# An attention and expert kernel: weighing of v by a list of pairs a slot, gates and expert choices at other places, six buffers of v

## The chip, the cores and the metric

The kernel runs on one core of one Trainium2 chip. Its time is the device time of one execution in microseconds (us); the time before is the median of three runs. One further execution was taken with the hardware profiler, and all durations below are from that one. Engines are named as the profile names them: PE is the matrix engine (PEld its weight loads), DVE the vector engine, ACT the scalar engine, POOL the GpSimd engine, SP the engine that issues most of the transfers. Each works through its own instructions in the order in which the program has them, and waits on semaphores for the others.

## The reference

Two blocks, the second fed by the first. Everything is float32.

```
scores = q @ k^T / sqrt(64)                      # (8 batches, 8 heads, 576, 576)
cum    = cumsum(max(s, 0))                       # (8, 8, 576)
scores = where(future, -1e9, scores + min(-(cum[i] - cum[j]), 0))
attn   = exp(scores - max);  attn /= sum(attn) + 1e-9
x      = heads of (attn @ v) side by side        # (8, 576, 512)

logits = x @ w_gate                              # 8 experts
local  = sigmoid(x @ w_local)
for b, s:  fresh = argmax(logits[b, s])
           e = fresh if s == 0 or local[b, s] < 0.5 else the e of the token before
           out[b, s] = softmax(logits[b, s])[e] * (relu(x[b, s] @ w1[e]) @ w2[e])
```

## The kernel before, in words

**Two stages.** The attention stage computes x and routes it: each token row of x is scattered to a table in device memory, ordered by expert. The expert stage takes units of up to 256 table rows that share an expert, multiplies them by that expert's w1 and w2, and scatters the results to the output.

**Attention by slots.** A *pair* n is two heads of one batch; there are 32, four a batch. The loop at L960 runs over 16 *slots* m of two pairs, 2m (even) and 2m + 1 (odd). In a slot PE first computes the scores of both pairs (`scores`, L854: tile `ps`, four parts a pair; ACT takes the exponential into `e`, POOL masks the diagonal blocks, L851), and then the values of both (`values`, L885). A pair's values come in two tiles, `po0` and `po6`, and each has one buffer. The sum over keys needs v weighed by the exponential of cum: `weigh(n)` (L837) writes it to one of four tiles `vg`, two DVE multiplications a pair (L845) and a small ACT copy (L842). v itself is loaded into `va`, of which there are four buffers (`p_v`, NV).

**Emptying and turning.** After each `po` tile DVE takes the reciprocal of the sums into `recs` (L902) and writes the scaled values to `xb` (L903). At a slot's end `turn` (L914) transposes both pairs into `xt` for the router, and then, before the change, `weigh` is called for the pairs 2m + 4 and 2m + 5.

**Places.** Other work is put into the slots by `plan(slot, place, f)`. Place 0 is after the even pair's scores, 1 after the odd pair's, 3 after the even pair's values, 4 after the odd pair's, 5 after turning and weighing. Since each engine keeps the program's order, the place decides what an instruction stands behind on its engine.

**The router.** Two batches form a group g, and there are four. With m = 4(g + 1), for the first three: `product` (PE, L213, at (m, 1)), `logits` (DVE, L222 to L231, at (m, 3)), `codes` and `turn1` (DVE, L238 to L267, at (m, 5)), `exps` (ACT, (m + 1, 1)), `turn2` (DVE, L274 to L289, (m + 1, 3)), `gates` (DVE, L321 to L332, (m + 1, 5)), `ranks` (PE, L297 and L298, (m + 2, 1)), `rows` (DVE, L306 to L313, (m + 2, 3)). Then the group's 18 scatters are laid out by the tuple STORES, whose entries are places, slot after slot from m + 2. A scatter is an indirect transfer that POOL issues (L345); at places 3, 4 and 5 a one-element copy of `recs` (L344) ahead of it makes POOL wait until DVE has got to that emptying. Scatters that STORES doesn't place go to the expert stage.

**Choosing units.** `assign_early(0)` and `assign_early(1)` (L407; `assign`, L376) choose the experts and rows of the first two and the next three units on DVE, from the counts so far: some 20 small instructions each. SP reads the result for the addresses of weights (`load`, L497) and rows (`fetch`, L517). The first stood at (10, 5), the second at (15, 0). The last group's first half has its product and logits at (14, 4). In the expert stage `run` (L613) has a list of its own: (u, c) is after the c-th column block of unit u's first layer.

**What holds buffers.** `xb` of batch 7 takes the buffer of batch 3, so its first emptying (pair 28, slot 14) waits for batch 3's scatters, the last of which is at (13, 5). The `kb` and `qb` of pairs 2m + 4 and 2m + 5 are requested inside slot m, behind a one-element DVE write (L762) that follows the emptying of the odd pair's `po0`.

Of the kernel before, what the change touches and what calls it, by code (L numbers as in the profile page):

```python
# [12 lines left out]
Alu = mybir.AluOpType  # L13
# [4 lines left out]
P = 128  # L18
B, H, S, DH = 8, 8, 576, 64
D = H * DH  # L20
E, F = 8, 1024
N = B * S
HP = H // 2
# [18 lines left out]
GB = 2  # L42
NG = B // GB
NC = GB * NJ
XW = 4 * 32 + 2
NV = 4
STORES = (((4, 5), (0, 1, 3, 4, 5), (0, 1, 3, 4, 5), (0, 1, 3, 4, 5), (0,)), ((4, 5, 5), (0, 1, 3, 4, 5), (0, 1, 3, 4, 5), (0, 1, 3, 4, 5)),
          ((4, 5), (0, 0, 1, 1, 3, 4, 5, 5)))
BX = 3
CAP = N + DH  # L50
ROWS = E * CAP + 2 * P
# [1 line left out]
DOUBLE, SINGLE, HALF, QUARTER = 2 * P, P, P // 2, P // 4  # L53
EARLY = (2, 3)
# [57 lines left out]
class Router:  # L112
# [294 lines left out]
    def assign_early(self, i):  # L407
        v = self.nc.vector
        self.counted()
        n = self.shifted("n0", 8)  # L410
        if i == 0:
            self.used, self.start, self.early = self.t("used", [P, E]), self.t("start", [P, E]), []
            v.memset(self.used, 0.0)
        v.tensor_tensor(n, n, self.used, op=Alu.subtract)
        v.tensor_scalar(self.start, self.used, float(DOUBLE), None, Alu.mult)
        of, used, _ = self.assign(f"a{i}", n, self.start, EARLY[i], DOUBLE)
        self.early.append(of)
        v.tensor_tensor(self.used, self.used, used, op=Alu.add)

    def assign_doubles(self):  # L420
        v = self.nc.vector
# [27 lines left out]
class Experts:  # L449
# [163 lines left out]
    def run(self, recs, wend, out_of):  # L613
        tc, ctx, nc, router = self.tc, self.ctx, self.nc, self.router
# [10 lines left out]
        last, first = NG - 1, sum(EARLY)  # L625
        self.banks = lambda name: self.ps_m.tile([P, 1, 512], F32, name=name, tag="m")

        def late_rows():
# [4 lines left out]
            self.puts += router.pads()  # L633

        todo = {
            (0, 2): [lambda: router.product(last, self.xts_of, self.banks, (1,)),
                     lambda: router.logits(last, (1,)), lambda: router.codes(last), lambda: router.exps(last),
                     lambda: router.turn1(last), lambda: router.turn2(last)],
# [17 lines left out]
            before[l] = two[i - 2] if i >= 2 else None  # L656
        self.load(1)
        self.turn_x(1)
        self.load(2)
        loaded, done, fetched, freed = [3, 3], (set(), set()), 2, False  # L660

        def ready(l, layer):
# [68 lines left out]
def attention(ctx, tc, q, k, v, s, wx, ident, recs, wend, router, experts):  # L731
# [4 lines left out]
    def pool(name, bufs, **kw):  # L736
        return ctx.enter_context(tc.tile_pool(name=name, bufs=bufs, **kw))

    once = pool("once", 1)
    p_in = pool("p_in", 4)  # L740
    p_v = pool("p_v", NV)
    p_e = pool("p_e", 2)
    p_x = experts.p_x
    p_x0 = pool("p_x0", 1)
# [21 lines left out]
    def load_v(n):  # L766
        if n >= NPAIR:
            return
        b, hp = divmod(n, HP)
        va = vs[n] = p_v.tile([P, NB, 2, DH], F32, name="va")  # L770
        nc.sync.dma_start(va.rearrange("p c h d -> p (c h d)"), v[b, hp].rearrange("p c h d -> p (c h d)"))
# [14 lines left out]
    load_qk(2)  # L786
    load_v(2)
    load_qk(3)
    load_v(3)
    router.projection(wx)  # L790
    wk = once.tile([P, NPAIR, G1 + NB, 2], F32, name="wk")
    nc.gpsimd.memset(wk[:TL, :, G1 + NF], 0.0)
# [44 lines left out]
    def weigh(n):  # L837

        if n >= NPAIR:
            return  # L840
        va, vg = vs.pop(n), vgs[n % NV]
        nc.scalar.copy(vg[:, :, :, VW - 2 : VW - 1].rearrange("p c h e -> p (c h) e"),  # L842
                       wk[:, n].rearrange("p c h -> p (c h)").unsqueeze(2))
        for to, c in ((slice(0, G1), G1), (slice(G1, G1 + NB), NB)):
            nc.vector.tensor_tensor(vg[:, to].rearrange("p c h e -> p (c h) e")[:, :, :DH],  # L845
                                    va[:, :c].rearrange("p c h e -> p (c h) e"),
                                    wk[:, n, to].rearrange("p c h -> p (c h)").unsqueeze(2).to_broadcast([P, c * 2, DH]),
                                    op=Alu.mult)
# [59 lines left out]
    def turn(n):  # L908

        b, hp = divmod(n, HP)  # L910
        bl = b % GB
        if hp == 0:
            xts[b] = (p_xt, experts.p_xt)[bl].tile([P, HP, 2, NJ, 32], F32, name=f"xt{bl}")
        nc.vector.transpose(xts[b][:, hp].rearrange("p d j t -> p j d t"), xs[b][:, :, :, 32 * hp : 32 * hp + 32])  # L914

    def of(g):
        return xts[g * GB], xts[g * GB + 1]

# [2 lines left out]
    def plan(slot, place, f):  # L921
        todo.setdefault((slot, place), []).append(f)

    for g in range(NG - 1):
        m = HP * GB // 2 * (g + 1)
        plan(m, 1, lambda g=g: router.product(g, of(g), banks))
        plan(m, 3, lambda g=g: router.logits(g))
        plan(m, 5, lambda g=g: (router.codes(g), router.turn1(g)))
        plan(m + 1, 1, lambda g=g: router.exps(g))
        plan(m + 1, 3, lambda g=g: router.turn2(g))  # L930
        plan(m + 1, 5, lambda g=g: router.gates(g, [xs[b] for b in range(g * GB, g * GB + GB)]))
        plan(m + 2, 1, lambda g=g: router.ranks(g, banks))
        plan(m + 2, 3, lambda g=g: router.rows(g))
        places = [(m + 2 + i, p) for i, ps in enumerate(STORES[g]) for p in ps]
        for c in range(NC):
            if c >= len(places):
                experts.puts.append(lambda after, g=g, c=c: router.scatter(g, c, after))
                continue
            i, p = places[c]
            after = {3: (2 * i, NJA), 4: (2 * i + 1, 0), 5: (2 * i + 1, NJA)}.get(p)  # L940
            after = after and recs[0:1, after[0], after[1], 0:1]
            plan(i, p, lambda g=g, c=c, after=after: router.scatter(g, c, after))
    m = NPAIR // 2
    plan(1, 5, router.constants)
    plan(2, 5, router.constants2)
    plan(2, 3, range_ends)
    plan(m - 6, 5, lambda: router.assign_early(0))
    for i in range(4):
        plan(m - 5 + i, 5, lambda i=i: experts.load(0, None, i))
    plan(m - 2, 0, lambda: (experts.fetch(0), experts.fetch(1)))  # L950
    plan(m - 2, 4, lambda: router.product(NG - 1, (xts[B - 2],), banks, (0,)))
    plan(m - 2, 4, lambda: router.logits(NG - 1, (0,)))
    plan(m - 1, 0, lambda: experts.turn_x(0))
    plan(m - 1, 0, lambda: router.assign_early(1))

    def at(slot, place):
        for f in todo.pop((slot, place), ()):
            f()

    for m in range(NPAIR // 2):  # L960
        pair = 2 * m, 2 * m + 1
        for n in pair:
            for u in range(len(UNITS)):
                if (n, u) == (0, 3):
                    key_exps()
                scores(n, u)
                if (n, u) == (1, 0):
                    key_weights()
                    weigh(0)
                    weigh(1)  # L970
            at(m, n - 2 * m)
        for n in pair:
            values(n, 0, NJA)()
            if n % 2:
                for i in pair:
                    load_qk(i + NV, i == n - 1)
                    if m:
                        load_v(i + NV + 2)
            values(n, NJA, NJ)()
            at(m, 3 + n - 2 * m)  # L980
        for n in pair:
            turn(n)
        for n in range(2 * m + (NV if m else 2), 2 * m + NV + 2):
            if not m:
                load_v(n + 2)
            weigh(n)
        at(m, 5)
    assert not todo
    experts.xb, experts.xts_of = [xs[B - 2], xs[B - 1]], of(NG - 1)
# [573 lines left out]
```

## Time and profile before

| What | us |
|---|---|
| median of three runs (lowest, highest) | 743.07 (742.19, 744.46) |
| the profiled execution | 742.65 |
| its span | 740.8 |
| attention stage, first values to the last values' end | 13.75 to 217.09 |
| expert stage on PE | 217.09 to 734.10 |
| last output rows | 734.10 to 740.8 |
| PE, DVE, ACT, POOL busy | 723.3, 259.1, 163.8, 212.1 |

The span runs from the first to the last recorded instruction. Slots of the attention stage start on PE at 19.74 (slot 1), 33.25, 44.99, 57.00, 71.06, 83.91, 96.36, 108.17, 122.22, 135.81, 148.27, 161.63, 175.85, 189.27 and 203.72 (slot 15). In the lists of groups and timelines a line names the source line, engine, operation, output and input tile and shapes, then how often; a bracket at the end says how long the engine was idle before it, and what ended that. A matrix multiplication of float32 shows as two records, so the 50 of a pair's values are "x100".

### The profile page before, as it was taken

To read this page: it belongs to the slowest core of one execution; us is meant where nothing else is said; L and a number is where in the kernel's file an instruction comes from. 1 tells how busy PE (TensorE), PEld (TensorE's weight loads), DVE (VectorE), ACT (ScalarE), POOL (GpSimd) and SP (SyncE) were. 2 spreads that over 40 slices of the span, in tenths; PEclk is the share of its full clock that TensorE was granted. 3 is DMA by queue.
4 is the path that set the end of the run, shared out by engine and by line. 5 is a ranking of instruction groups with operands and counts; after the bars stand their busy time and mean duration, and the time that the engine had idled before them with its cause. 6 is when DMAs were issued, how large, how long until landed. Compare 5 with 4: busy or idle time off the path is not lost.

```text
span 740.8 us, 16102 instructions
## 1 busy us (share of the span) xinstructions
PE 723.3 (98%) x6509; PEld 496.2 (67%) x6509; DVE 259.1 (35%) x704; ACT 163.8 (22%) x327; POOL 212.1 (29%) x453
## 2 busy tenths in 40 slices
PE   8999999999999999999999999999999999999996
PEld 6788788878876756756756376446735576647674
DVE  4756866886774741101110411230041001050110
ACT  4554545354331101101101010101100011101110
POOL 3553477687574434520110101010001001010110
PEclk9999999999999999999999999999999999999999
DMA  6553555567669878688457969996999955899000
GB/s 214 186 191 116 187 165 184 186 213 271 222 198 423 275 306 295 261 341 259 156 180 231 379 244 424 316 388 224 419 345 379 414 199 214 288 393 346 31 15 33
DMA packets 57348, 187.28 MB, mean 253 GB/s; under 512 B 11885, under 2 KB 31597, under 8 KB 49840
## 3 DMA queue, kind: packets, MB, share of 16 engines
q1 hardware_dynamic: 50464, 166.06, 62.8%
q0 software_dynamic: 6800, 20.09, 7.1%
q8 instruction: 53, 0.87, 0.5%
q14 instruction: 31, 0.25, 0.1%
HBM read 165.50 MB, written 20.88 MB: 252 GB/s over the span
## 4 chain that ended last, share of the span: by engine, by line
PE 87%; DVE 8%; POOL 1%; DMA 1%; issue 1%; ACT 1%; POOLq 0%; DVEq 0%; ACTq 0%
PE yp L600 35%; PE hp L576 31%; PE po L895 9%; PE ps L865 7%; PE hp L567 4%; DVE vg L845 1%; PE lp L213 1%; DVE xb L903 1%; DVE xt L914 1%; DMA table<-xb,idx 1%; DVE l L228 1%; ACT e L866 1%; POOL e L851 1%; PE warm L800 1%; DVE recs L902 0%
## 5 line engine op out<-in xcount | busy, mean ns | idle before, releaser
L600 PE MATMUL yp<-w2b,hT 128*128 128x512 f32 (+2 forms) x752 | 259.3, 593 | 0.0
L576 PE MATMUL hp<-xT,w1b 128*128 128x256 f32 (+1 forms) x1216 | 233.2, 352 | 0.0
L576 PEld LDWEIGHTS hp<-xT,w1b 128*128 128x128 f32 x1216 | 206.2, 190 | 32.5 <-issue 7.5
L600 PEld LDWEIGHTS yp<-w2b,hT 128*128 128x128 f32 (+2 forms) x752 | 107.9, 167 | 141.0 <-issue 139.6
L605 POOL DMA_INDIRECT out_dram<-y,gi x37 | 36.5, 986 | 416.8 <-DVE y L603 397.8
L578 ACT ACTIVATE hT<-hp 128x256 f32<-128x256 f32 (+1 forms) x152 | 54.0, 355 | 429.2 <-PE hp L576 429.2
L603 DVE TENSOR_SCALAR y<-yp,gi 128x512 f32<-128x512 f32 x37 | 27.6, 746 | 304.7 <-PE yp L600 298.3
L895 PE MATMUL po<-vg,e 128*64 128x66 f32 x3200 | 98.8, 223 | 8.7 <-DVE recs L902 7.1
L895 PEld LDWEIGHTS po<-vg,e 128*64 128x64 f32 x3200 | 95.8, 138 | 11.4 <-issue 7.0
L866 ACT ACTIVATE e<-ps 128x768 f32<-128x768 f32 (+1 forms) x128 | 95.5, 852 | 23.2 <-PE ps L865 23.2
L865 PE MATMUL ps<-qb,kb 64*128 64x192 f32 (+4 forms) x768 | 94.7, 400 | 0.2 <-ACT e L866 0.2
L851 POOL TENSOR_SCALAR_AFFINE_SELECT e<-e 128x256 f32<-128x256 f32 (+1 forms) x160 | 73.2, 483 | 51.2 <-ACT e L866 50.1
L865 PEld LDWEIGHTS ps<-qb,kb 64*128 64x128 f32 x768 | 65.7, 188 | 29.1 <-ACT e L866 15.0
L345 POOL DMA_INDIRECT table<-xb,idx x54 | 53.2, 985 | 18.3 <-issue 15.3
L587 DVE STREAM_TRANSPOSE hT<-hs 32x256 f32<-32x256 f32 x64 | 27.9, 436 | 74.8 <-ACT hs L569 74.0
L845 DVE TENSOR_TENSOR vg<-va,wk 128x256 f32<-128x256 f32 x64 | 44.5, 755 | 2.3 <-DMA va<-in_v_dram 2.2
L546 DVE STREAM_TRANSPOSE xT<-xq 128x1024 f32<-128x1024 f32 (+1 forms) x23 | 23.6, 1028 | 18.6 <-DMA xq<-table 18.3
L902 DVE RECIPROCAL recs<-po 128x12 f32<-128x12 f32 x64 | 13.4, 209 | 44.6 <-PE po L895 44.5
L567 PE MATMUL hp<-w1b,xT 128*32 128x512 f32 (+1 forms) x224 | 28.3, 594 | 0.0
L842 ACT COPY vg<-wk 128x14 f32<-128x14 f32 x32 | 6.7, 217 | 81.9 <-PE po L895 81.4
L903 DVE TENSOR_TENSOR xb<-po,recs 128x384 f32<-128x384 f32 (+1 forms) x48 | 22.0, 458 | 2.5 <-DMA table<-xb,idx 0.9
L567 PEld LDWEIGHTS hp<-w1b,xT 128*32 128x32 f32 (+1 forms) x224 | 8.1, 114 | 17.7 <-issue 17.6
(231 smaller groups left out, 205.2 us busy)
## 6 DMA issues: line engine op xcount, KB each, us to landing
w1b<-in_w_dram SPq DMA_DIRECT2D x29, 2048.0 KB, 10.3
w2b<-in_w_dram SPq DMA_DIRECT2D x29, 2048.0 KB, 10.7
va<-in_v_dram SPq DMA_DIRECT2D x32, 320.0 KB, 5.6
kb<-in_k_dram SPq DMA_DIRECT2D x32, 288.0 KB, 4.4
qb<-in_q_dram SPq DMA_DIRECT2D x32, 288.0 KB, 5.0
xq<-table SPq DMA_DIRECT2D x56, 130.0 KB, 10.9
w1b<-in_w_dram SPq DMA_DIRECT2D x4, 512.0 KB
w2b<-in_w_dram SPq DMA_DIRECT2D x4, 512.0 KB, 5.9
```

The source lines that it names most:

```text
L345: put = self.nc.gpsimd.indirect_dma_start(out=self.halves, in_=src, element_offset=0, in_offset=None, out_offset=bass.IndirectOffsetOnAxis ...
L567: mm(ps[d, :], lhsT=xT[:, k, d], rhs=self.ws[l][0][:, k, c * 512 : c * 512 + 512], start=(k == 0), stop=(k == DK - 1))
L576: mm(ps[:, :w], lhsT=self.ws[ls[0]][0][:, k, c * P : c * P + P], rhs=xT[:, k, :w], start=(k == 0), stop=(k == DK - 1))
L578: nc.scalar.activation(self.hT[u][:, c, :w], ps[:, :w], Act.Relu)
L600: mm(ps[d, :], lhsT=hT[:, k, n * P + d.start : n * P + d.stop], rhs=self.ws[l][1][:, k, :], start=(k == 0), stop=(k == FK - 1))
L605: put = nc.gpsimd.indirect_dma_start(out=self.out[:, :], out_offset=bass.IndirectOffsetOnAxis(ap=gi.bitcast(I32)[:, n, 0:1], axis=0), in_= ...
L845: nc.vector.tensor_tensor(vg[:, to].rearrange("p c h e -> p (c h) e")[:, :, :DH], va[:, :c].rearrange("p c h e -> p (c h) e"), wk[:, n, to ...
L851: nc.gpsimd.affine_select(out=ap, in_=ap, compare_op=Alu.is_ge, fill=0.0, base=base, pattern=n, channel_multiplier=-1)
L865: mm(ps[:, h, at : at + z - a], lhsT=kb[d, key : key + P], rhs=qb[d, a:z], start=True, stop=True)
L866: nc.scalar.activation(e, ps, Act.Exp, scale=scale)
L895: mm(po[d, j - j0, :], lhsT=weights_of(n, c, j, h), rhs=vgs[n % NV][:, c if j < 2 * G1 else G1 + c, h, :], start=(c == 0), stop=(c == last))
L903: nc.vector.tensor_tensor(xb[:, j0:j1, :, 32 * hp : 32 * hp + 32], po[:, :, :DH].rearrange("p j (g i) -> p j g i", g=2), rec[:, :, 0].unsq ...
```

## The change

- `weigh` goes by a list. WEIGHED gives for each slot the last pair that is weighed by its end: slots 0 to 15 weigh 2, 4, 2, 2, 0, 2, 2, 4, 0, 2, 2, 4, 0, 3, 1 and 0 pairs (pairs 0 and 1 are weighed in the prologue as before). Before, slot 0 weighed four, and slots 1 to 13 two each.
- At a slot's end weighing now comes ahead of turning, but in slots 3, 7, 11 and 15 turning stays ahead.
- `va` has six buffers (NVA). v of the pairs 0 to 5 is requested in the prologue, and inside slot m that of 2m + 6 and 2m + 7.
- `gates` moves from (m + 1, 5) to (m + 2, 3), behind `rows`.
- `assign_early(0)` moves from (10, 5) to (11, 3), and no longer subtracts or adds a start that is zero. `assign_early(1)` moves from (15, 0) into the expert stage, behind the first column block of unit 0, and the load of unit 2 with it.
- The last group's half product moves from (14, 4) to (15, 1), and its logits to (15, 3).
- STORES: one scatter fewer at the start of group 0, at slot 6, and two for three at slot 10 and no place 4 there or in slot 14; in exchange slot 10 has two at place 0 and slot 13 two at place 1.

```diff
+NVA = 6
+WEIGHED = (3, 7, 9, 11, 11, 13, 15, 19, 19, 21, 23, 27, 27, 30, 31, 31)
-STORES = (((4, 5), (0, 1, 3, 4, 5), (0, 1, 3, 4, 5), (0, 1, 3, 4, 5), (0,)), ((4, 5, 5), (0, 1, 3, 4, 5), (0, 1, 3, 4, 5), (0, 1, 3, 4, 5)),
-          ((4, 5), (0, 0, 1, 1, 3, 4, 5, 5)))
+STORES = (((5,), (0, 1, 3, 4, 5), (0, 1, 3, 4, 5), (0, 1, 3, 4, 5), (0, 0)), ((5, 5), (0, 1, 3, 4, 5), (0, 1, 3, 4, 5), (0, 1, 1, 3, 4, 5)),
+          ((5, 5), (0, 0, 1, 1, 3, 4, 5, 5)))
...
         if i == 0:
-            self.used, self.start, self.early = self.t("used", [P, E]), self.t("start", [P, E]), []
-            v.memset(self.used, 0.0)
-        v.tensor_tensor(n, n, self.used, op=Alu.subtract)
-        v.tensor_scalar(self.start, self.used, float(DOUBLE), None, Alu.mult)
-        of, used, _ = self.assign(f"a{i}", n, self.start, EARLY[i], DOUBLE)
+            self.start, self.early = self.t("start", [P, E]), []
+            of, self.used, _ = self.assign("a0", n, None, EARLY[0], DOUBLE)
+        else:
+            v.tensor_tensor(n, n, self.used, op=Alu.subtract)
+            v.tensor_scalar(self.start, self.used, float(DOUBLE), None, Alu.mult)
+            of, used, _ = self.assign(f"a{i}", n, self.start, EARLY[i], DOUBLE)
+            v.tensor_tensor(self.used, self.used, used, op=Alu.add)
         self.early.append(of)
-        v.tensor_tensor(self.used, self.used, used, op=Alu.add)
...
         todo = {
+            (0, 0): [lambda: router.assign_early(1), lambda: self.load(2)],
...
         self.load(1)
         self.turn_x(1)
-        self.load(2)
...
-    p_v = pool("p_v", NV)
+    p_v = pool("p_v", NVA)
...
-    load_v(3)
+    for n in range(3, NVA):
+        load_v(n)
...
+    def turns(pair):
+        for n in pair:
+            turn(n)
...
-        plan(m + 1, 5, lambda g=g: router.gates(g, [xs[b] for b in range(g * GB, g * GB + GB)]))
         plan(m + 2, 1, lambda g=g: router.ranks(g, banks))
         plan(m + 2, 3, lambda g=g: router.rows(g))
+        plan(m + 2, 3, lambda g=g: router.gates(g, [xs[b] for b in range(g * GB, g * GB + GB)]))
...
-    plan(m - 6, 5, lambda: router.assign_early(0))
+    plan(m - 5, 3, lambda: router.assign_early(0))
...
-    plan(m - 2, 4, lambda: router.product(NG - 1, (xts[B - 2],), banks, (0,)))
-    plan(m - 2, 4, lambda: router.logits(NG - 1, (0,)))
     plan(m - 1, 0, lambda: experts.turn_x(0))
-    plan(m - 1, 0, lambda: router.assign_early(1))
+    plan(m - 1, 1, lambda: router.product(NG - 1, (xts[B - 2],), banks, (0,)))
+    plan(m - 1, 3, lambda: router.logits(NG - 1, (0,)))
...
                     load_qk(i + NV, i == n - 1)
-                    if m:
-                        load_v(i + NV + 2)
+                    load_v(i + NVA)
...
-        for n in pair:
-            turn(n)
-        for n in range(2 * m + (NV if m else 2), 2 * m + NV + 2):
-            if not m:
-                load_v(n + 2)
+        last = m % HP == HP - 1
+        if last:
+            turns(pair)
+        for n in range(WEIGHED[m - 1] + 1 if m else 2, WEIGHED[m] + 1):
             weigh(n)
+        if not last:
+            turns(pair)
         at(m, 5)
```

## The prediction

> **What bounds the kernel now.** I read the page's busy shares first, then the windows by stage, then the waits of PE, then PE's and DVE's timelines at each wait. The expert stage, as one window (us, then busy time of PE, PEld, DVE, ACT, POOL):
>
> ```profile
> 217.09:734.10 517.01, 516.97 (x2265) 324.14 (x2262) 104.43 (x264) 58.97 (x161) 81.07 (x148) 1.00 0.76 281
> ```
>
> PE is idle 0.04 us of 517, so the change can save nothing there and only lose. What can be won is PE's idle time in the attention stage, to 217.09. PE's waits:
>
> ```profile
> PE po L895 <- DVE recs L902: 7.1, 6, 1.6
> PE po L895 <- POOL low L135: 1.5, 1, 1.5
> ```
>
> They lie here in PE's timeline (start, length; idle before in brackets):
>
> ```profile
> 30.18 3.14 PE L895 MATMUL po<-vg,e 128*64 128x66 f32 x100 [1.54 <-POOL low L135]
> ...
> 80.84 3.14 PE L895 MATMUL po<-vg,e 128*64 128x66 f32 x100 [0.88 <-DVE recs L902]
> ...
> 132.74 3.14 PE L895 MATMUL po<-vg,e 128*64 128x66 f32 x100 [1.62 <-DVE recs L902]
> ...
> 158.57 3.14 PE L895 MATMUL po<-vg,e 128*64 128x66 f32 x100 [1.40 <-DVE recs L902]
> ...
> 186.20 3.14 PE L895 MATMUL po<-vg,e 128*64 128x66 f32 x100 [1.45 <-DVE recs L902]
> ...
> 199.20 3.14 PE L895 MATMUL po<-vg,e 128*64 128x66 f32 x100 [0.32 <-DVE recs L902]
> ...
> 214.02 3.14 PE L895 MATMUL po<-vg,e 128*64 128x66 f32 x100 [1.40 <-DVE recs L902]
> ```
>
> Seven stalls, 8.61 us, in slots 1, 5, 9, 11, 13, 14, 15, always before the odd pair's values. Each of the two `po` tiles has one buffer, so the odd pair waits for DVE to empty the even pair's. The first is put down to POOL, but DVE finishes that emptying at 30.04 too. DVE just before the stall of slot 5:
>
> ```profile
> 72.24 1.43 DVE L914 STREAM_TRANSPOSE xt<-xb 128x576 f32<-128x576 f32 x2
> 73.59 2.81 DVE L845 TENSOR_TENSOR vg<-va,wk 128x256 f32<-128x256 f32 x4
> 76.33 0.29 DVE L238 TENSOR_REDUCE mx<-l 128x18 f32<-128x144 f32 x1
> ...
> 80.13 0.56 DVE L903 TENSOR_TENSOR xb<-po,recs 128x384 f32<-128x384 f32 x1
> ```
>
> Two turns, two weighings (2.73) and the codes (3.6) are queued before an emptying that the values waited for at 79.96. It is a backlog in one slot; over slots 2 to 15 DVE is busy 135.9 of 183.8 us.
>
> **What the Trainium skill says.** "PSUM — Partial Sum Buffer", section Engine vs sequencer instructions: the queues of ScalarE, VectorE and GpSimd are strict FIFO. The trace agrees: the emptying at 80.13 stands behind work that PE doesn't need then. "SBUF — State Buffer", section Who interferes with whom: a DVE instruction with two SBUF inputs contends with a GpSimd instruction that reads SBUF. Weighing has two, and five masks take 2.97 us beside one and 1.74 without:
>
> ```profile
> 152.57 1.74 POOL L851 TENSOR_SCALAR_AFFINE_SELECT e<-e 128x256 f32<-128x256 f32 x5
> ...
> 178.99 2.97 POOL L851 TENSOR_SCALAR_AFFINE_SELECT e<-e 128x256 f32<-128x256 f32 x5
> ```
>
> "Perfetto Trace Analysis", section Optimization Strategy: repeating gaps on the engine that should be saturated can mean too few buffers; here it is `po`'s one, which the change leaves alone.
>
> **Frame for the sums.** A slot of PE: scores 5.76, then values 3.07 a pair, 11.8 in all; a product adds 2.31 (1.5 for half), ranks 0.72. So the odd pair wants its tile 8.83 after the slot's start. On DVE: emptying 0.83 and 0.60, turns of two pairs 1.36, one weighing 1.36 (two took 2.73 beside masks, 2.12 without).
>
> **Part by part, gains.** Slots 5, 9, 13 (0.88 + 1.62 + 1.45): slots 4, 8, 12 now weigh nothing, so DVE is ready 2.73 earlier than 80.0, 131.9, 185.3. The emptying then follows the even pair's first values (7.3 after the slot's start) and is over 0.7 before it is wanted. Gone: 3.95.
> Slot 11 (1.40): choosing the first units, 152.44 to 157.60, moves behind the emptying of pair 22. Gone. Six of its 21 instructions go too (0.07, 0.31, 0.38, 0.39, 0.32, 0.17; about 1.5 us of starts), so 3.7 remains. With the four weighings that slot 11 now has, from its start: emptyings to 9.5, choice to 13.2, emptyings to 14.6, turns to 16.0, pairs 24 to 27 to 21.4, pair 24 emptied at 22.2. PE wants it at 11.8 + 5.76 + 2.31 + 3.07 = 22.9. 0.7 to spare, which the product of slot 12 pays for.
> Slot 15 (1.40): the second choice, 208.67 to 213.14, leaves for the first unit. Half a product comes in, whose PE time only changes slot, and half of the logits (2.2), behind the emptying of pair 30. Gone.
> Slot 1 (1.54): DVE stood 2.23 for v of pair 4 and then weighed 4 and 5. These now come at slot 1's end, from loads issued in the prologue. Gone. Slot 2 then starts behind 0.6 + 4 x 1.36 + 1.36 = 7.4; pair 4 is empty at 8.3 against 8.83. Slot 8 has the same and a product more.
> Nothing: turning behind weighing (in slots 3, 7, 11, 15 turning stays first, as the product of the next slot needs it); six v buffers (v is loaded three slots ahead; 5.6 us to land; two loads ahead of wx, which slot 4 reads first; without that cover, their length). Gates behind ranks lengthen slots 6, 10, 14 on DVE by 1.95, but after the even pair's tiles are emptied; the loads of q and k behind that emptying start 3 us later, and their readers start two slots on, about 4 us after they land.
>
> **Losses.** Slot 14: pair 28's emptying writes over rows that the last scatter of slot 13 reads.
>
> ```profile
> 198.50 0.56 DVE L903 TENSOR_TENSOR xb<-po,recs 128x384 f32<-128x384 f32 x1 [0.85 <-DMA table<-xb,idx]
> ```
>
> That scatter starts 15.9 after slot 13's start (175.85) and lands 6.28 on, at 22.2. With turn2 1.1 earlier, it starts at 14.8 and lands at 21.1; DVE passes 0.5 later, pair 29's values start at 22.3. But slot 13 is 1.45 shorter, and PE wants them at 11.8 + 5.76 + 0.72 + 3.07 = 21.3. The stall grows from 0.32 to about 1.0.
> POOL: a scatter at place 4 or 5 waits for an emptying and holds up the next slot's masks. With gates ahead of it, slot 6's go-ahead comes about 2.0 into slot 7 (before 0.3); one scatter instead of two ends at 3.8 (before 2.9). Five masks of 1.74 to 2.97 end at 5.5 to 6.8; values start at 5.76 and reach the last masked tile a microsecond later. Stall 0 to 0.1. Slot 11, behind two scatters, end at 5.0: masks to 6.8 to 8.0, stall 0 to 1.2. Slots 10 and 15, with two scatters between the pairs' masks: 0 to 1.2, 0 to 1.6. Between 0 and 4.1 together; I take 1.0, as masks and weighings overlap only in part. It could not gain: POOL set no stall before.
> The first unit: DVE does the second choice (4.5) ahead of the last logits, which starts them about 1 us later; DVE idled 7.39 before the unit's output. SP's load of unit 2, and the fetches behind it, wait for the choice, some 6.5 us later than at 218.7. The load's second half took 25.3 from 219.3 and is read from 288.7, its first half from 274.6. Unit 0's last quarter goes out behind the first fetches, about 29 after slot 13's start, lands 5.9 on, and PE reads it at about 40. So nothing; without the cover it would be the lateness itself, up to 6.5.
>
> **Sum.** -8.61 + 1.0 + 1.0 = -6.6. The profiled execution took 742.65 (span 740.8), so 736.0; the median of the three runs is 0.42 above it: 736.4 us, 0.9% less.
>
> **Rivals.** (1) POOL becomes the bound: all masks at the slow rate, 4.1 of stalls beside slot 14's 1.0, so -3.5 and 739.6. For it: POOL is already busy 10.6 of 11.8 in slot 7, and its even masks there ended at 102.0, 0.1 before PE came for them. Against it: weighings cover only part of the masks, and slots 9 and 13 weigh nothing ahead of theirs now.
> (2) The backlog moves along: two weighings took 3.30 at worst (110.13), so four take 6.6 and not 5.4. Slot 2 then stalls by 0.7 and slot 12 by 0.5 (slot 8 has 2.8 to spare): 737.6.
> (3) Slower, by one chain: slot 13's last scatter, then pair 28's emptying and SP's fetch of unit 0, both of which wait for its landing. For it: this chain carries the path at 191.73 already. It decides once landing takes over 6.28 + 6.6 + 2.2 = 15.1 us, and then gives 745.3 and up. Against it: the longest landing of a scatter from 150 to 250 was 10.5.
> (4) The edit doesn't act, because what PE waited for was another engine: 743.1. The row for POOL speaks for it; DVE's emptyings, which end within 0.15 of all seven restarts, speak against it.
>
> **Chances.** A measurement of this kernel tells about 0.3% (2.2 us) from no change. Forecast 0.68, (1) 0.17, (2) 0.04, (4) 0.06, (3) or a late load of the first units 0.05. Faster takes the first three less 0.02 of (1) that runs past 740.8: 0.87; same 0.08; slower 0.05. Range: from 734.2 (all 8.6 won, and 0.3 of scatter between runs) to 740.2, which takes in (1) and (2); the forecast's own is 734.2 to 738.
>
> **What would show it.** After: no DVE wait of PE in slots 1, 5, 9, 11, 13, 15; one near 0.7 to 1.2 in slot 14; attention ends about 210.5; the expert stage stays near 517.0. Waits for masks in slots 7, 10, 11, 15 are (1); DVE waits in slots 2, 8, 12 are (2); a gap of PE beyond 217, in unit 0 or 2, would make the prediction wrong.

## The result, and the profile after

The changed kernel takes 740.41 us (median of six runs, 739.31 to 741.15) and the kernel before, beside it, 742.96 (741.32 to 744.46): a ratio of 0.9966, with a 95% interval of 0.9950 to 0.9982. It is faster by 2.5 us or a third of a per cent. Predicted were 6.6 us; the direction is right, the size is not, and 740.4 lies 0.2 above the range. The profiled execution took 741.15, with a span of 739.4; its attention stage ends at 215.5, where about 210.5 was forecast.

The expert stage is what it was. The window of 517 us that answers to the one shown before starts 1.59 us earlier and has PE idle for 0.03 us (columns as before: window, length, busy time and count of PE, PEld, DVE, ACT, POOL, then granted clock, busy share of the DMA engines and GB/s):

```profile
215.50:732.50 517.00, 516.97 (x2264) 324.13 (x2262) 107.53 (x283) 58.99 (x161) 81.62 (x150) 1.00 0.76 281
```

So all that happened, happened in the attention stage. PE's largest waits after the change (total us, times, longest):

```profile
PE po L899 <- issue: 7.0, 5, 2.0
PE warm L804 <- DVE xb L783: 1.5, 1, 1.5
PE po L899 <- DVE recs L906: 0.6, 1, 0.6
```

Before, DVE kept PE from the values for 7.1 us and the row put down to POOL for 1.5. Both are gone but for 0.6. In their place stands a row that was not there: 7.0 us in five waits with the releaser "issue", the page's word for time in which the engine waited for nothing that the profile shows. PE's timeline has them here (start, length, count, idle before):

```profile
79.26 2.44 PE L899 MATMUL po<-vg,e 128*64 128x66 f32 x76 [1.29 <-issue]
105.90 2.25 PE L899 MATMUL po<-vg,e 128*64 128x66 f32 x69 [1.98 <-issue]
172.76 1.62 PE L899 MATMUL po<-vg,e 128*64 128x66 f32 x47 [1.43 <-issue]
186.40 1.44 PE L899 MATMUL po<-vg,e 128*64 128x66 f32 x41 [1.45 <-issue]
198.02 3.14 PE L899 MATMUL po<-vg,e 128*64 128x66 f32 x100 [0.64 <-DVE recs L906]
212.44 3.13 PE L899 MATMUL po<-vg,e 128*64 128x66 f32 x98 [0.88 <-issue]
```

The "issue" stalls lie in slots 5, 7, 12, 13 and 15. The counts tell a lot. A stall for `po` comes ahead of a pair's values, so x100 follows it, as in every row before and in slot 14 here. The new ones leave x76, x69, x47 and x41 (and x98 in slot 15): they come *inside* a pair's values, where no tile changes hands.

**What resumes at these places.** Counted over all recorded PE instructions (weight loads, matmuls, and PE's semaphore instructions), PE resumes at numbers 3009, 4034, 6849, 7362 and 8386. Their distances are 1025, 2815, 513 and 1024, within one of multiples of 256; the remainder is .754 to .758 of 256 each time. Below, a *block* is the 256 instructions between two such places, and a stall *at the remainder* is one at such a place. The page has a DMA queue that no line of the kernel uses, with 53 packets of 16 KB (its row: packets, MB, share of the DMA engines), and PE has some 13,000 recorded instructions, 51 times 256:

```profile
q8 instruction: 53, 0.87, 0.5%
```

This suggests that a packet holds 256 instructions of PE, and that PE stands still where the next packet is late. Slot 5 in windows of one microsecond:

```profile
73.00:74.00 1.00, 1.00 (x12) 0.67 (x8) 0.90 (x4) 1.00 (x3) 0.65 (x3) 1.00 0.96 245
74.00:75.00 1.00, 1.00 (x34) 0.93 (x32) 0.72 (x3) 1.00 (x2) 0.59 (x2) 1.00 0.89 338
75.00:76.00 1.00, 1.00 (x42) 1.00 (x38) 0.19 (x1) 0.75 (x4) 0.71 (x3) 1.00 0.84 324
76.00:77.00 1.00, 1.00 (x42) 1.00 (x40) 0.60 (x2) 0.00 (x0) 0.07 (x1) 1.00 0.24 87
77.00:78.00 1.00, 0.98 (x34) 0.89 (x31) 0.63 (x4) 0.00 (x0) 0.00 (x0) 1.00 0.01 5
78.00:79.00 1.00, 0.00 (x0) 0.00 (x0) 0.91 (x5) 0.00 (x0) 0.00 (x0) 1.00 0.00 0
```

Until about 76.5 the loads of q, k and v fill the DMA engines. The packet starts at 76.83, as they run dry, and lands at 77.77; PE resumes at 79.26, 1.49 later. In the five cases PE resumes 1.34 to 1.62 us after the landing. PE had passed the previous place with this remainder at 73.88, 2.96 ahead of the packet's start; in the five cases this is 2.3 to 3.6 us. Values use up 256 instructions in 3.7 to 3.9 us (a pair's 100 matmul records, each with a weight load, take 3.07). For slot 7: 3.60 until the packet starts, 0.97 to land, 1.37 until PE resumes, 5.94 in all. PE had work for 3.95 of them, and the other 1.98 is the stall. All these parts are read from one trace and have to add up; they show where the time goes if the packet is asked for when PE passes into the block ahead of it. Whether that is the cause, the experiments have to tell.

The Trainium skill, "Runtime: NRT & Kernel Launch", section Instruction fetch mechanics, says that instructions are refilled in blocks of 16 KB, 256 instructions, fetched over a DMA queue while the current one runs. This trace agrees on the size. On the cost of a boundary the page says "mostly hidden". That holds here for most of the 51, but five cost 0.88 to 1.98 us each.

Slot 7 before and after, windows of the kernel before first. PE's values begin at 102.2 before and at 99.9 after, but the loads come to their end near 104 in both:

```profile
102.00:103.00 1.00, 1.00 (x36) 0.93 (x33) 0.00 (x0) 1.00 (x2) 0.84 (x3) 1.00 1.03 400
103.00:104.00 1.00, 1.00 (x42) 1.00 (x40) 0.21 (x1) 0.34 (x1) 0.98 (x4) 1.00 0.90 345
104.00:105.00 1.00, 1.00 (x42) 1.00 (x40) 0.58 (x2) 0.00 (x0) 0.98 (x4) 1.00 0.25 86
```

```profile
102.00:103.00 1.00, 1.00 (x42) 1.00 (x39) 0.34 (x1) 0.00 (x0) 0.95 (x4) 1.00 1.04 411
103.00:104.00 1.00, 0.91 (x31) 0.77 (x27) 0.55 (x2) 0.22 (x1) 0.90 (x1) 1.00 0.48 181
104.00:105.00 1.00, 0.00 (x0) 0.00 (x0) 0.00 (x0) 0.00 (x0) 0.83 (x3) 1.00 0.38 129
```

The packet starts at 103.76 before and at 103.56 after. Before, PE reached the block at 105.98, 1.24 after the landing, with no stall; after, it wanted it at 103.9.

### The profile page after: what moved, and what is told of

It reads as the page before. It is cut to its first block, busy times and chain, and to the rows that moved or that the text cites. A ratio compares the mean times of both kernels' runs of the same rounds, so it can differ in the third digit from the quotient of the medians.

```text
span 739.4 us, 16096 instructions
## 1 busy us (share of the span) xinstructions
PE 722.6 (98%) x6509; PEld 495.8 (67%) x6509; DVE 252.2 (34%) x698; ACT 161.6 (22%) x327; POOL 206.2 (28%) x453
## 4 chain that ended last, share of the span: by engine, by line
PE 94%; issue 1%; DVE 1%; DMA 1%; POOL 1%; ACT 0%; POOLq 0%; DVEq 0%
PE yp L603 35%; PE hp L579 31%; PE po L899 12%; PE ps L869 11%; PE hp L570 4%; PE lp L215 1%; DMA table<-xb,idx 1%; PE warm L804 1%; POOL table L347 0%; ACT e L870 0%; DVE xb L907 0%; POOL gap L346 0%; PE pos L299 0%; POOL e L855 0%; DVE recs L906 0%
## 5 line engine op out<-in xcount | busy, mean ns | idle before, releaser
L855 POOL TENSOR_SCALAR_AFFINE_SELECT e<-e 128x256 f32<-128x256 f32 (+1 forms) x160 | 66.7, 441 | 52.1 <-ACT e L870 50.7
L849 DVE TENSOR_TENSOR vg<-va,wk 128x256 f32<-128x256 f32 x64 | 41.1, 707 | 0.0
L918 DVE STREAM_TRANSPOSE xt<-xb 128x576 f32<-128x576 f32 x24 | 17.1, 751 | 0.0
```

Source lines behind the costliest of these rows:

```text
L855: nc.gpsimd.affine_select(out=ap, in_=ap, compare_op=Alu.is_ge, fill=0.0, base=base, pattern=n, channel_multiplier=-1)
```

## The experiments

Three theories. **A**: PE runs out of instructions, because the packet with the next ones waits behind loads that are already under way. **B**: PE waits there for masks or exponentials, and the trace does not show it. **C**: a packet always takes too long for a block that is all values, whatever else the DMA carries.

The runs came in four sets, each on one chip beside the kernel before. In the second set the kernel before took 743.1 us, as at first; in the other three 753.5, 751.6 and 752.8. There PE made pauses of about 0.4 us, mostly two or three in a row 0.75 us apart, in values and at no fixed remainder. Slots without a pause could be slower too (slot 8 of the changed kernel: 14.86 us in the fourth set, 14.06 in the second), and so was the start of the expert stage. The changed kernel in the fourth set, PE's timeline:

```profile
161.02 0.35 PE L899 MATMUL po<-vg,e 128*64 128x66 f32 x3 [0.45 <-issue]
161.77 1.53 PE L899 MATMUL po<-vg,e 128*64 128x66 f32 x44 [0.40 <-issue]
```

What makes the pauses was not examined. They blur times, so in these sets I go by the stalls at the remainder, and compare times within a set. Ratios are to the kernel before in the same set.

**Without the loads** (first set). It leaves out the loads of q, k and v once each buffer has been filled, so later heads get other data and the routing is another.

```diff
 def load_qk(n, behind=False):
+        if n >= NV:
+            ins[n] = ins[n - NV]
+            return
...
 def load_v(n):
+        if n >= NVA:
+            vs[n] = va_of[n % NVA]
+            return
```

> The changed kernel with q, k and v loaded for the first four pairs (v: six) only; later pairs read these tiles again. It leaves out those loads, so later heads get other data, and with them the routing is another; only the attention stage is compared. Theory A (PE runs out of instructions): PE's instruction stream comes in packets of 16 KB, 256 instructions, on a DMA queue of its own; in the changed kernel all five stalls of PE in the middle of a values block resume at the same remainder of 256 recorded PE instructions (11.754, 15.758, 26.754, 28.758, 32.758 blocks) and about 1.4 us after a late packet has landed, and each late packet starts just as the loads of q, k and v run dry. Without these loads the packets start at once: the stalls in slots 5, 7, 12 and 13 (1.29 + 1.98 + 1.43 + 1.45 = 6.15 us) go, that in slot 15 (0.88, beside loads of weights) may stay, and the attention stage ends 6.1 to 7.0 us earlier, at 208.5 to 209.4 us in place of 215.5. Theory B (PE waits there for masks or exponentials, and the trace does not show it): ACT and POOL do the same work, the five stalls stay and the stage ends at 215 to 216. Theory C (a packet always takes too long for a block that is all values, whatever the other queues carry): the stalls stay as well, each after a packet that starts 2 to 4 us after its block was asked for.

No stall at the remainder is left; the gaps of PE in the values are pauses of 0.3 to 0.45. The end of the stage, expected at 209, came at 220.9. The changed kernel in the fourth set, where the kernel before took as long, ended it at 222.5 and has two stalls at the remainder, of 2.3 us together. So the stalls go with the loads, against B and C, but the size expected for a chip without pauses is not tested by this run.

**Loads earlier** (first and second set). A slot's loads, and the one-element write ahead of them, go behind the emptying of the even pair's first tile.

```diff
-            if n % 2:
+            if n % 2 == 0:
                 for i in pair:
-                    load_qk(i + NV, i == n - 1)
+                    load_qk(i + NV, i == n)
```

> The changed kernel with a slot's loads of q, k and v issued, and the memset that they wait for placed, behind the emptying of the even pair's first tile in place of the odd pair's: 3.1 us earlier in every slot. Theory A: the loads have landed 3.1 us earlier relative to the next slot's values, so the packet asked for as the values start is no longer behind them: stalls in slots 5, 7 and 13 go (4.7 us), slot 12's shrinks or goes (1.4), slot 15's (0.88) stays as it hangs on loads of weights. Time 734.3 to 736.5, attention ends at about 209.5 to 211. Theories B and C: no stall depends on when the loads are issued; time 740.4 within 1.

First set: 750.24, ratio 0.9955 (0.9941 to 0.9968), and no stall at the remainder, but pauses in many blocks. Expected were 734 to 736 on a chip of 743, so by time alone this run decides nothing; it was run again beside the changed kernel.

> The changed kernel as it is, beside the others of this set on one chip, as the earlier experiments ran on a chip where the kernel before took 753.5 us. All theories: 0.996 to 0.998 of the kernel before. Theory A: stalls of 0.8 to 2 us in the middle of values blocks at the remainder .754 to .758 of 256 recorded PE instructions in slots 5, 7, 12, 13 and 15.

> The changed kernel with the loads of q, k and v 3.1 us earlier in every slot, once more, beside the changed kernel itself. In the first run no stall at the remainder .754 to .758 was left, but pauses of some 0.4 us every 0.75 us stood in many blocks, which that chip may have put into the changed kernel too. Theory A: at least 3 us less than the changed kernel on the same chip (ratio to before 0.988 to 0.993), and none of the five stalls. Theory B or C: the same time as the changed kernel within 1 us.

The changed kernel in the second set: 740.16, ratio 0.9965 (0.9954 to 0.9976). It has the stalls in slots 7, 12, 13 and 15 (1.15, 1.55, 1.73, 0.97), and none in slot 5 this time: the packet there started 1.60 after PE had passed the place ahead, not 2.96.

```profile
PE po L899 <- issue: 5.4, 4, 1.7
```

With earlier loads: **732.92**, ratio 0.9866 (0.9846 to 0.9886), 7.2 us less. That is more than the 4 to 6 first expected, since slot 15's stall goes as well, and since a slot that loses a stall shortens by 0.1 to 0.3 us more than the idle time shown (slot 7 goes from 13.16 to 11.75 us, with a stall of 1.15). PE's largest waits:

```profile
PE warm L804 <- DVE xb L783: 1.5, 1, 1.5
PE cps L825 <- ACT xb L817: 0.3, 1, 0.3
PE po L899 <- DVE recs L906: 0.3, 1, 0.3
```

The row "issue" is gone whole. Slot 5 in windows:

```profile
74.00:75.00 1.00, 1.00 (x21) 0.79 (x18) 0.89 (x4) 1.00 (x3) 0.47 (x2) 1.00 0.07 16
75.00:76.00 1.00, 1.00 (x42) 1.00 (x40) 0.22 (x1) 1.00 (x5) 0.53 (x2) 1.00 0.00 0
76.00:77.00 1.00, 1.00 (x42) 1.00 (x40) 0.70 (x2) 0.21 (x3) 0.53 (x2) 1.00 0.00 0
77.00:78.00 1.00, 1.00 (x42) 1.00 (x40) 0.29 (x3) 0.00 (x0) 0.00 (x0) 1.00 0.00 0
```

As PE passes into the block ahead, at 74.33, the DMA engines are all but idle; the packet starts 0.48 later. The attention stage ends at 207.6 in place of 214.4, with 0.27 of PE's 8.6 left. No work of PE was removed. C needs a packet to be slow whatever the queues carry, and here it isn't.

> The changed kernel as it is, for comparison with the others of this set on one chip. On a chip without pauses 740 us and four or five stalls at the remainder .754 to .758; on a chip with them about 748 to 751 us, and some of these stalls smaller, since PE takes its instructions more slowly there.

> The changed kernel with the loads of q, k and v 3.1 us earlier, beside the changed kernel. On a chip without pauses 7 us less than that, as measured. On a chip with pauses: theory A alone says 1 to 4 us less, as PE's pauses leave the packets more time; if pauses come in place of the stalls, nothing.

Beside the changed kernel on a chip with pauses (fourth set) it took 750.43, ratio 0.9977 (0.9965 to 0.9989), against 752.67, 0.9988 (0.9973 to 1.0003): 2.2 us less, within the 1 to 4 expected. Not all of it need be the loads. No stall at the remainder is left, of two with 2.3 us together, but the attention stage of the profiles ends only 1.2 us earlier (221.3, not 222.5), as there are more pauses. The rest lies in the expert stage, where the changed kernel's profile shows a granted clock of 0.98 from 217 to 300 us and this one 1.00.

**Loads later** (third and fourth set): the same lines behind the odd pair's second tile.

```diff
-            if n % 2:
-                for i in pair: ...
             values(n, NJA, NJ)()
+            if n % 2:
+                for i in pair: ...
```

> The changed kernel with the loads of a slot 1.2 to 1.5 us later, behind the emptying of the odd pair's second tile. Theory A: packets asked for at the start of the values wait longer: the stalls of slots 5, 7, 12 and 13 grow by about that much each and one near 1 appears in slot 3, whose margin was nothing: 10 to 14 us of such stalls in all, time 744 to 748 where the changed kernel takes 740.2. Theories B and C: no change, 740.

> The changed kernel with the loads of a slot 1.2 to 1.5 us later. Theory A: 4 to 8 us more than the changed kernel on a chip without pauses, with stalls in slots 1, 3, 5, 7, 12 and 13; 2 to 6 us more on a chip with them. Theories B and C: no difference.

Third set: 753.49, ratio 1.0030 (1.0010 to 1.0050), with stalls at the remainder in slots 1, 3, 5, 7 and 14 (0.95, 1.58, 0.28, 1.63, 0.50): 4.9 us where 10 to 14 were expected, and none in slots 12 and 13. Fourth set: 754.97, 1.0030 (1.0015 to 1.0044), 2.3 us more than the changed kernel beside it. PE's timeline there, at the remainder:

```profile
18.46 1.39 PE L899 MATMUL po<-vg,e 128*64 128x66 f32 x40 [0.91 <-issue]
55.96 0.92 PE L899 MATMUL po<-vg,e 128*64 128x66 f32 x24 [1.58 <-issue]
81.84 2.44 PE L899 MATMUL po<-vg,e 128*64 128x66 f32 x76 [1.38 <-issue]
108.52 2.26 PE L899 MATMUL po<-vg,e 128*64 128x66 f32 x69 [1.80 <-issue]
180.01 1.62 PE L899 MATMUL po<-vg,e 128*64 128x66 f32 x47 [0.86 <-issue]
208.42 1.39 PE L899 MATMUL po<-vg,e 128*64 128x66 f32 x40 [0.41 <-issue]
```

That is 6.9 us, in slots 1, 3, 5, 7, 12 and 14. The changed kernel beside it has two of them, and 2.3 us:

```profile
78.78 2.44 PE L899 MATMUL po<-vg,e 128*64 128x66 f32 x76 [0.43 <-issue]
105.50 2.26 PE L899 MATMUL po<-vg,e 128*64 128x66 f32 x69 [1.88 <-issue]
```

So the stalls follow the time of the loads in both directions. Of the six expected places slot 13 has none again, and slot 14 was not expected.

**Blocks shifted.** PE instructions that nobody reads, ahead of slot 0, move the places where blocks begin to an earlier point of the program: first 124 of them, in place of one of the two warm-up products, then 88 in place of both.

```diff
-    warm_up(2)
+    small = banks("warm")[:, 0]
+    for i in range(24):
+        mm(small[:64, :66], lhsT=zero[:, :64], rhs=zero[:, :66], start=True, stop=True)
```

> The changed kernel with one of the two warm-up products of the prologue replaced by 32 small ones, 128 x 64 by 66 columns, that nobody reads: about 124 more PE instructions ahead of slot 0, in time in which PE waits for q and k anyway, so nothing else moves. Theory A: the places at which PE passes from one packet of instructions to the next come 124 instructions earlier in the program. In slots 5, 7 and 13 the block that was all values then takes in scores, and their stalls shrink or go; in slots 9, 10 and 11, whose blocks were mixed and had no stall, a block becomes all values (3.7 us of PE) while the loads still run, and stalls of 1 to 2 us appear there, in the middle of values blocks. The sum over the stage stays of the same order, 5 to 11 us, and the time comes to 738 to 745. Theories B and C both differ: B leaves the stalls in slots 5, 7, 12, 13 and 15 at the same matmuls (time 740.4, within 0.5); C moves them too, but to every slot with an all-values block, early slots 1 to 3 too, with a like size everywhere.

> The changed kernel with 124 more PE instructions ahead of slot 0 once more, since pauses of 0.4 us in many blocks blurred the first run of it. Theory A: stalls of 0.5 us or more at the remainder .754 to .758, in slot 3 (1.1 in the first run) and in slots 9 to 12, none in slots 5, 7 and 13, whose blocks are now mixed; ratio to before 0.994 to 1.002. Theory B: stalls in slots 5 (in one of two runs), 7, 12, 13, 15 as in the changed kernel, ratio 0.9965.

> The changed kernel with both warm-up products of the prologue replaced by 24 small ones, 88 PE instructions more, in the same 3.7 us, so slot 0 starts when it did. Theory A: blocks of instructions begin 88 instructions earlier in the program; slots 5 and 7 then have mixed blocks and no stall, slots 9, 10 and 11 get blocks that are all values and with them stalls of 0.3 to 1.5 us, slots 12 to 14 keep theirs at another place, all at the remainder .754 to .758. Sum 4 to 9 us, time within 3 us of the changed kernel. Theory B: the stalls stay in slots 7, 12, 13 and 15.

With 124 (first and third set): 1.0038 (1.0022 to 1.0053), and 1.0053 (1.0036 to 1.0070) when run again; but the small products took 5.4 and 4.9 us, not the 1.9 of the product they replace, which put slot 1 off to 21.7 and more, so some 2 us of the loss is not from stalls. With 88 (fourth set): 1.0027 (1.0014 to 1.0040), 1.9 us more than the changed kernel beside it. Here too the small products took 5.4 us and not 3.8, and slot 1 starts at 20.24 and not at 19.46, so 0.8 of the 1.9 is the later start. The places are what counts. The stalls at the remainder are those of slots 3 and 12, first with 88, then with 124 in its second run:

```profile
55.54 2.20 PE L901 MATMUL po<-vg,e 128*64 128x66 f32 x67 [1.93 <-issue]
178.13 2.90 PE L901 MATMUL po<-vg,e 128*64 128x66 f32 x90 [0.75 <-issue]
```

```profile
55.59 2.72 PE L902 MATMUL po<-vg,e 128*64 128x66 f32 x85 [1.00 <-issue]
177.53 3.62 PE L902 MATMUL po<-vg,e 128*64 128x66 f32 x108 [0.67 <-issue]
```

Slots 5 and 7 have none. In slots 3 and 12 the counts behind the stall can be held against those of the kernel with later loads, x24 and x47: with 88 more instructions PE resumes 43 matmuls earlier in both (x67, x90), with 124 more 61 earlier (x85, x108). A matmul comes with a weight load, so these are half of 88 and of 124, to one. The stall stays at a place in the stream of instructions, not at a matmul, a mask or a tile; this settles it against B. The expected stalls in slots 9 and 10 did not come, and in slot 11 only 0.26, with 124; slots 13 and 14, which were to keep theirs, have none. The sums are 2.7 us with 88 and 1.5 to 1.9 with 124, where 4 to 9 and 5 to 11 were expected: which blocks are late was foreseen in part only.

> The kernel with earlier loads (732.9 us, no stall of this kind) and the 124 more PE instructions ahead of slot 0. Theory A: with the loads landed before the values start, it matters little where a block of instructions begins: below 1.5 us of such stalls in all, 732.5 to 734.5. If the phase of the blocks had been the cause by itself, it would cost as much here as in the changed kernel, some us.

With the loads early (third set), the shift by 124 leaves no stall at the remainder. The ratio, 0.9998 (0.9983 to 1.0012), misses the expected 733 us: that chip has its pauses, and slot 1 starts some 2 us later. The time decides nothing.

**The gates back** at the end of the slot before (first and third set).

```diff
-        plan(m + 2, 3, lambda g=g: router.gates(...))
+        plan(m + 1, 5, lambda g=g: router.gates(...))
```

> The changed kernel with one part undone: the gates of a group are again at the end of the slot before the ranks, as in the kernel before, and no longer between the ranks' rows and the emptying of the odd pair's first tile. In slots 6 and 10 the memset that lets the loads go then comes about 1.9 us earlier relative to PE. Theory A: in slot 7 the loads have landed when the values ask for their packet, and its stall of 1.98 goes or falls below 0.5; those of slots 5, 12, 13 and 15 stay. Time about 738.5 (737.9 to 739.2), if DVE's longer queue at the end of slot 5 costs nothing. Theories B and C: slot 7's stall stays, time 740.4 or more.

> The changed kernel with the gates back at the end of the slot before, once more, for the same reason. Theory A: slot 7's stall (1.15 to 1.98 in the changed kernel) goes; those of slots 12, 13 and 15 stay. In the first run PE waited 1.25 us for DVE in slot 14 (0.25 to 0.64 in the changed kernel), which takes most of it back: 739 to 740.5 us where the changed kernel takes 740.2.

Slot 7's stall, 1.15 to 1.98 in three profiles of the changed kernel, is gone in the first run and 0.28 in the second. The times, ratios 0.9960 (0.9947 to 0.9973) and 0.9962 (0.9949 to 0.9975), have no changed kernel in the same set; DVE's wait in slot 14 was 1.25 and 0.49. Of the stalls that were to stay, slot 12's did (0.97, 0.46) and slot 5's in the second run (0.42); those of slots 13 and 15 are not there. So it is shown that the moved gates make slot 7's packet later, and not what undoing them is worth.

**Two runs of the kernel before** (second set): its loads earlier in the same way; and one part of the change alone, the list for weighing with six buffers of v and turning behind weighing.

> The kernel before, its loads of q, k and v moved in the same way (issued behind the emptying of the even pair's first tile). Theory A: in the kernel before the late packets hide behind waits for DVE, so earlier loads win next to nothing: ratio 0.997 to 1.001, and the DVE waits of PE in slots 5, 9, 11, 13 and 15 (0.88, 1.62, 1.40, 1.45, 1.40) are all there. If instead the load times set the end in the kernel before too, it wins 3 us or more (0.996 or less).

739.88, ratio 0.9953 (0.9938 to 0.9969). It won 3.2 us, where theory A had expected next to nothing. PE's timeline:

```profile
78.80 3.14 PE L895 MATMUL po<-vg,e 128*64 128x66 f32 x100 [0.89 <-DVE recs L902]
130.65 3.14 PE L895 MATMUL po<-vg,e 128*64 128x66 f32 x100 [1.62 <-DVE recs L902]
156.48 3.14 PE L895 MATMUL po<-vg,e 128*64 128x66 f32 x100 [1.38 <-DVE recs L902]
183.94 3.14 PE L895 MATMUL po<-vg,e 128*64 128x66 f32 x100 [1.44 <-DVE recs L902]
211.21 3.14 PE L895 MATMUL po<-vg,e 128*64 128x66 f32 x100 [1.39 <-DVE recs L902]
```

The five waits for DVE are all there, as expected. Gone are slot 1's (1.54; v of pair 4, for which DVE stood, is requested behind these loads) and slot 14's (0.32). That is 1.9 us of idle time. The lengths of the slots account for more: slot 1 is 1.8 us shorter and slot 14 0.5, and slots 3, 7 and 12, where the kernel before took its packets with nothing to spare, 0.3, 0.1 and 0.2. So late packets seem to have cost the kernel before about half a microsecond already, without a stall that the waits would list. Together this is 2.8 us, as the profiles differ (742.65 and 739.88); 0.4 of the medians' difference is left over.

```diff
+WEIGHED = (3, 7, 9, 11, 11, 13, 15, 19, 19, 21, 23, 27, 27, 30, 31, 31)
-    p_v = pool("p_v", NV)
+    p_v = pool("p_v", NVA)
...
+        for n in range(WEIGHED[m - 1] + 1 if m else 2, WEIGHED[m] + 1):
             weigh(n)
```

> One part alone: the kernel before with the list of pairs a slot for weighing, six buffers of v and turns behind the weighing; gates, choices of early units, scatters and the last product stay where they were. The waits of PE for DVE in slots 1, 5, 9 and 13 (5.5 us) go, those in slots 11 and 15 stay. Theory A: packets become late in slots 5 and 13, whose blocks of instructions lie as in the changed kernel, and give back 1.3 and 1.45 us; slot 9's block is mixed and gives nothing back; slot 7 has no stall, as its loads are not behind the gates. Net -2.7 us or so, ratio 0.995 to 0.998. Prediction's theory (all DVE waits are won): -5.5 us, ratio 0.9926.

742.60, ratio 0.9990 (0.9974 to 1.0005): the list alone makes no difference that can be told, where 2.7 us were expected. The waits for DVE in slots 1, 5, 9 and 13 are gone, 5.5 us. PE's timeline has 4.2 us of late packets in their place, among them these, and the wait for DVE in slot 15:

```profile
172.19 1.62 PE L898 MATMUL po<-vg,e 128*64 128x66 f32 x47 [0.61 <-issue]
185.83 1.44 PE L898 MATMUL po<-vg,e 128*64 128x66 f32 x41 [1.45 <-issue]
199.54 1.39 PE L898 MATMUL po<-vg,e 128*64 128x66 f32 x40 [0.98 <-issue]
214.03 3.14 PE L898 MATMUL po<-vg,e 128*64 128x66 f32 x100 [2.82 <-DVE recs L905]
```

Slot 13's wait for DVE of 1.45 has become a packet's of 1.45. A had placed the rest badly: slot 5 has 0.42 and not 1.3, and slots 7, 12 and 14 have 0.60, 0.61 and 0.98 where none was expected. Nor had A counted slot 15, where DVE's 1.40 became 2.82: the list puts a weighing (1.37) at the end of slot 14, ahead of the second choice, which in this kernel still stands there.

## Why the prediction was wrong in size

**What bounds the kernel** held: the change did nothing to the expert stage, and the seven stalls were waits for DVE. The row for POOL was DVE's too; it went when DVE no longer stood there for v.

**The gains**, slot by slot, were right as far as DVE goes: no wait for it is left in slots 1, 5, 9, 11, 13 and 15. The four weighings ahead of slots 2, 8 and 12 make no stall, so rival 2 is out.

**The losses** taken at 1.0 + 1.0 were 0.64 for slot 14 (0.25 in the second profile, of the changed kernel run again) and 0.12 for masks, in slot 11; these were put too high, by over 1 us, which by luck offset part of the term that was missing. Rival 1's time, 739.6, is near the measured one, but not its mechanism.

**The step that failed** is the paragraph on what costs nothing, at "the loads of q and k behind that emptying start 3 us later, and their readers start two slots on", and with it the sum, which counts all 8.61 us of DVE's waits as won. It asked who reads the loads, and not what else moves on the same DMA engines. PE's own instructions do, and they are used not two slots on but within 4 us. Where a wait for DVE went, the values came earlier, and the loads did not keep pace. The write that lets slot 6's loads go, in the kernel before and after the change:

```profile
96.17 0.06 DVE L762 MEMSET kb<- 1x1 f32 x1
95.47 0.06 DVE L765 MEMSET kb<- 1x1 f32 x1
```

Slot 7 starts at 96.36 before and at 94.09 after, so seen from PE the go-ahead comes 1.6 us later, behind the gates. The same holds for slot 12, where the prediction overlooked it: the first choice now stands ahead of slot 11's go-ahead, which comes at 159.75, 1.2 after slot 12's start, and came at 160.99, 0.6 ahead of it. Slot 12's stall is 1.43 with that, and 0.61 in the run with the list alone, which leaves the choice where it was.

In the kernel before this was near its limit already: in slots 3, 7 and 12 PE reached its block 1.2 to 1.3 us after the packet's landing, about as soon as in any case of these traces. In slot 13 the packet landed at 186.41, so that it was of use from about 187.75 (1.34 later); PE came for it at 187.92, and without its wait for DVE of 1.45 would have come at 186.47. So that wait covered one of 1.3 us for the packet.

So the sum from the two first profiles is 8.61 of waits gone, less 7.03 for late packets, 0.64 for slot 14 and 0.12 for masks: 0.82 won. The attention stage ends 1.59 earlier; the rest is the start of slot 1, at 18.90 in place of 19.74, and 19.87 in the second profile of the changed kernel, so that it is no gain of the change. With that second profile the same sum is 8.61 less 5.40, 0.25 and 0.13: 2.8 won, and measured beside it are 2.9. The term that the prediction had at nothing is 5.4 to 7.0 us. With the loads moved out of its way, the gains of the forecast come out: 0.27 of 8.6 us of stalls are left. The time, 732.9 us, is even below the 734.4 of the forecast without its losses: slots that lost a stall shortened by somewhat more than the idle time that the prediction counted, and slots 3, 7 and 12, which had none, by 0.5 us together.

**The rivals.** 3 and 4 did not come; none of the four held a late transfer of instructions. The sign that the prediction gave for being wrong, a gap of PE beyond 217, was looked for in the wrong stage.

Shown by runs: the stalls follow the time of the loads, earlier, later and left out; and their places follow the count of instructions. Argued from the trace alone: that a packet is asked for as PE enters the block ahead of it. PE's records give that moment roughly at best: in the attention stage of the kernel before, one packet (slot 12) started 0.9 us ahead of it. Left open: the pauses of 0.4 us, with which earlier loads win 2.2 us at most and not 7.2; and by what rule one block's packet is late and another's not, as several of the expected places were missed.

## What to carry over

When a wait is taken from an engine, ask what else it had been covering there, instructions included: here a stretch of small instructions used up 256 of them in under 4 us, and their refill shared the DMA engines with bulk loads. A wait in the middle of a run of like instructions, put down to "issue", is worth counting against the instruction number; where the places agree modulo a packet's size, try moving the loads and not the work. Here two lines that put the loads 3 us earlier were worth 7.2 us beside the change's 2.9, and gave the fastest kernel of all, 732.92 us, on a chip without pauses.

## What was not expected of the hardware

- In the changed kernel's five late cases a packet of 16 KB on the instruction queue took 0.9 to 1.0 us but started 2.3 to 3.6 us after PE had passed into the block ahead. It started near the end of the loads: in slots 5 and 7 within 0.4 us of the last load packet's start, in slots 12, 13 and 15 0.8 to 1.4 us ahead of it; in the kernel with earlier loads it mostly started 0.2 to 0.5 us after that for blocks that are all values.
- PE began no block sooner than 1.2 us after its packet had landed, in any of the traces.
- The kernel before took 743.1 us in one set and 752.8 in another, 1.3% more. There the changed kernel has pauses of PE of 0.4 us, while the clock column of its attention stage stands at 1.00.
